# Reordering early loads and a store in a chunked state-space scan followed by a two-layer SiLU block

## The chip, the cores and the metric

The kernel runs on one core of a Trainium2 chip. The metric is the device time of one execution in microseconds (us), lower is better. TensorE (PE) multiplies matrices, VectorE (DVE), ScalarE (ACT) and GpSimd (POOL) do elementwise work, and SyncE (SP) mostly issues DMA transfers. Each engine works through its own queue in order.

## The reference

The first part is a Mamba-2 style scan over 4 batches, 8 heads, 768 positions, head size 32 and state size 16. For one chunk of positions:

```python
la = log(clip(a, 1e-6, 1.0)); cum = cumsum(la)
M = (C @ B.T) * exp(cum[:, None] - cum[None, :]) * causal
y = M @ x + (C @ state) * exp(cum)[:, None]
state = exp(sum(la)) * state + sum_j outer(B[j], x[j]) * exp(cum[-1] - cum[j])
```

The second part takes y as a matrix of 3072 tokens by 256 and computes `h = y @ w_in` (256 by 2048), `g = h * sigmoid(h)` and `out = g @ w_out` (2048 by 256). Everything is float32.

## The kernel before

The scan works in twelve units of 256 positions, three for each batch, numbered 0 to 11. Two units make one panel of 512 tokens for the second part, so there are six panels, P = 0 to 5. Panel 0 (units 0 and 1) is multiplied in plain float32 while its weights arrive; the later panels use weights and activations that are split into three parts, in the loop over `step(s)`. A hand-written order holds from the first instruction to the end of panel 0: the straight list of calls after the function definitions, then the list `steps`, then the texts "m0 ..." to "m5 ...". All engines receive their work in the order of these calls.

The weights come in sixteen blocks of 512 KB: blocks 0 to 7 of `w_in`, blocks 8 to 15 of `w_out`. This text counts them from 0, so "block five" in the short description of the change, which counts from one, is block 4. `load_w(n)` issues the load of block n on SP's queue into one of six buffers of the pool `quad`. `w_size(n)` is two ACT instructions that read the raw block (wu at L189, wv at L192). `w_bits(n)` is three DVE instructions and a POOL addition (L203 to L208) that give the usable block w. `f_s1(u, j)` multiplies block j with the scan result xf of unit u, eight matmuls (L531), and applies SiLU on ACT (gT, L534). Its PSUM tile hp has two buffers, so a product waits for the SiLU of the product before the last. `f_s2(j)` is the second layer of panel 0 (L544).

For a unit u of the scan: `f_TP` or `f_T` transposes B and C; `f_T2` makes ce from C (ACT, L408); `f_G` is the product of B and C (L442); scans over a on DVE give the decay matrix E (L356) and the prefix products pfx (L348); `f_B` scales B (BT, L380); `f_C` scales C (cw, L412); `f_D0` multiplies BT with x (L428); `f_M` (L448), `f_S` (L460, L462) and `f_SM` (L469) make the masked matrix and the states; `f_Y` (L482, L491) and `f_X` (L501) give xf. E and BT need the decays spread over partitions: for units 0 to 2 they come from products with `ach`, or from a copy `a_first`; from unit 3 on they come back from memory. For these POOL clamps a (`f_A2`, L273 and L275) after its load (`f_A1`), and `f_A3` stores it to the memory tensors `a_in` and `a_zero` with three SP issues (L280 to L282). `load_pa(u)` (L106) reads `a_in`, and `load_ab(u)` (L113) reads `a_zero` into ab, a tile with a single buffer, so it waits for the scans of the unit before. `load_n(u, i)` (L125) loads B (i = 0) or C (i = 1) with positions on partitions, `load_t` (L135) in another layout, `load_x` (L143) loads x, `load_bcx` both or some. `f_P0` (L344) clamps a for the prefix products of units 0 to 2 on POOL.

In the text of `steps`, each entry is `(u, j, work)`: first `f_s1(u, j)`, then the work, where `b3` is `w_bits(3)`, `s4` is `w_size(4)`, `r7` is `load_w(7)`, and `2:T2` calls `stage(2, ...)` with one letter for each function:

```python
steps = ((1, 0, "2:P1 s3"), (1, 1, "b3 s4 2:T2"), (0, 2, "2:BCa r7 b4 s5"), (1, 2, "2:DSsM r8 r9"),
```

In `stage` the letter `a` means `load_ab(u + 1)`.

Of the kernel before, what the change touches and what calls it, by code (L numbers as in the profile page):

```python
# [33 lines left out]
def kernel(  # L34
# [22 lines left out]
    nc = tc.nc  # L57
# [28 lines left out]
    def block(name, dtype=FP32):  # L86

        return blk.tile([128, 512], dtype, name=name, tag="blk", bufs=NB)
# [12 lines left out]
    def at(u):  # L101
        return u // UPB, u % UPB * UT

    def load_pa(u, q):
        PZ[u] = pz if u != 3 else block("pz3")[:, 0:4 * Q + 4].rearrange("p (c t) -> p c t", c=4)
        q.dma_start(out=PZ[u].rearrange("p c t -> p (c t)"),  # L106
                    in_=a_in[:, 4 * u - NC0:4 * u - NC0 + 4].rearrange("h (o c) t -> h o (c t)", o=1).to_broadcast([H, N, 4 * Q + 4]))

    def load_ab(u, q):
        ab[u] = loads.tile([128, 2, H, Q], FP32, name="ab")  # L110
        src, n = (a_first, 4 * u) if u < UPB else (a_zero, 4 * u - NC0)
        for c in range(2):
            q.dma_start(out=ab[u][64 * c:64 * c + 64].rearrange("p k h t -> p k (h t)"),  # L113
                        in_=src[n + c:n + 4:2].rearrange("(o k) h t -> o k (h t)", o=1).to_broadcast([64, 2, H * Q]))

    def load_n(u, i, q, ks=(0, 1)):
        b, t0 = at(u)
        if i == 1:
            if u not in tbc:
                tbc[u] = block("tbc0")[:, 0:256].rearrange("p (k h n) -> p k h n", k=2, h=H)  # L120
        elif u not in bn:
            bn[u] = (block("bn0")[:, 0:256].rearrange("p (k h n) -> p k h n", k=2, h=H) if u in (0, 1, 3) else
                     loads.tile([128, 2, H, N], FP32, name="bn"))
        for k in ks:
            q.dma_start(out=(bn, tbc)[i][u][:, k], in_=(B, C)[i][b, :, t0 + 128 * k:t0 + 128 * k + 128].rearrange("h p n -> p h n"))  # L125

    def load_t(u, i, q):
        b, t0 = at(u)
        if u == 0:
            tbc[u] = block("tbc0").rearrange("p (i e r n) -> p i e r n", i=2, e=2, r=8)  # L130
        elif u not in tbc:
            tbc[u] = loads.tile([128, 2, 2, 8, N], FP32, name="tbc")
        src = (B, C)[i]
        for g in range(4):
            q.dma_start(out=tbc[u][32 * g:32 * g + 32, i],  # L135
                        in_=src[b, 2 * g:2 * g + 2, t0:t0 + UT].rearrange("e (t r) n -> t e r n", r=8))

    def load_x(u, q, ks=(0, 1)):
        b, t0 = at(u)
        if u not in xt:  # L140
            xt[u] = loads.tile([128, 2, H, D], FP32, name="xt", bufs=2)
        for k in ks:
            q.dma_start(out=xt[u][:, k], in_=x[b, :, t0 + 128 * k:t0 + 128 * k + 128].rearrange("h p d -> p h d"))  # L143

    def load_bcx(u, what="bcx"):
        if "c" in what:
            if 0 < u < UPB:
                load_n(u, 1, nc.sync)
            else:
                load_t(u, 0, nc.sync)  # L150
                load_t(u, 1, nc.sync)
        if "b" in what:
            load_n(u, 0, nc.sync)
        if "x" in what:
            load_x(u, nc.sync)

    def load_unit(u):
        load_pa(u, nc.sync)
        load_bcx(u, "bc")
        load_ab(u, nc.sync)  # L160
        load_x(u, nc.sync)
# [10 lines left out]
    def two(t):  # L172
        return t.rearrange("p (k f) -> p k f", k=2)

    def load_w(n, q):
        j = n % 8
        src = wi[:, :, j * WF:(j + 1) * WF] if n < 8 else wo[:, 2 * j:2 * j + 2]
        if src.dtype == FP32:
            w32[n] = block("w32")
            q.dma_start(out=two(w32[n]), in_=src)  # L180
            return
        t = raw[n] = quad.tile([128, 2, WF, 2], U32, name="raw", tag="quad")
        q.dma_start(out=t.rearrange("p k f two -> p k (f two)"), in_=src.bitcast(U32))
# [86 lines left out]
    def f_A2(first):  # L270

        r = slice(0, NC1)
        nc.gpsimd.tensor_scalar(out=(acl if first else acz)[r], in0=acl[r], scalar1=1.0, scalar2=1e-6, op0=ALU.min, op1=ALU.max)  # L273
        if not first:
            nc.gpsimd.memset(acz[r, :, 0:1], 0.0)  # L275

    def f_A3():

        r = slice(0, NC1)
        nc.sync.dma_start(out=a_in[:, :, 0:1].rearrange("h c t -> c h t"), in_=misc[r, 0:H].rearrange("p (h t) -> p h t", t=1))  # L280
        nc.sync.dma_start(out=a_in[:, :, 1:].rearrange("h c t -> c h t"), in_=acl[r])
        nc.sync.dma_start(out=a_zero, in_=acz[r])  # L282
# [58 lines left out]
    def f_P0(u, engine):  # L341
        src = pa[u].rearrange("p (c t) -> p c t", t=Q)
        PZ[u] = (pz, pz1, pz)[u]
        engine.tensor_scalar(out=PZ[u][:, :, 1:], in0=src, scalar1=1.0, scalar2=1e-6, op0=ALU.min, op1=ALU.max)  # L344
# [16 lines left out]
    def f_Ab(u, k, hs=slice(0, H), bank=acc):  # L361
        t = ab[u, k, hs.start] = bank("ab").rearrange("p (h t) -> p h t", t=Q)
        nc.tensor.matmul(out=t[:, hs].rearrange("p h t -> p (h t)"),
                         lhsT=sel[:A1, 2 * u + k].rearrange("r c m -> r (c m)"),
                         rhs=ach[:A1, hs].rearrange("r h t -> r (h t)"), start=True, stop=True)
# [17 lines left out]
    def f_T(u, i):  # L383
        t = (BH, CT)[i][u] = sc.tile([128, UT], FP32, name=("bh", "ct")[i])
        nc.vector.transpose(out=t.rearrange("p (t r) -> p r t", r=8), in_=tbc[u][:, i].rearrange("p e r n -> p r e n"))
        if i == 1:
            tbc.pop(u)
# [17 lines left out]
    def f_T2(u, e):  # L405
        if e == 0:
            CE[u] = sc.tile([128, 2, UT], FP32, name="ce")
        nc.scalar.activation(CE[u][:, e], CT[u], AF.Copy, scale=par[:, e:e + 1])  # L408

    def f_C(u, engine=nc.vector):  # L410
        CW[u] = sc.tile([128, UT], FP32, name="cw")
        engine.tensor_tensor(out=CW[u].rearrange("p (c t) -> p c t", t=Q),  # L412
                             in0=CT.pop(u).rearrange("p (c t) -> p c t", t=Q), in1=PFX[u][:, :, 1:], op=ALU.mult)
# [32 lines left out]
    def f_M(u, k):  # L446
        m = E[u].rearrange("p k (g e) t -> p k g (e t)", e=2)
        nc.vector.tensor_tensor(out=m[:, k], in0=DP[u][:, :, 128 * k:128 * k + 128], in1=m[:, k], op=ALU.mult)  # L448
# [244 lines left out]
                in_=r[32 * q:32 * q + 32].rearrange("p (b d) -> p b d", d=32))  # L693


    f_P0(0, nc.gpsimd)
    load_n(1, 0, nc.gpsimd)
    f_Ab(0, 0, slice(0, 4))
    f_Ab(0, 0, slice(4, 8))
    f_Ab(0, 1, slice(0, 4), half)  # L700
# [24 lines left out]
    f_M(0, 0)  # L725
    w_size(0, "u")
    f_C(0, nc.gpsimd)
    load_n(1, 1, nc.gpsimd)
    f_S(0)
    f_SM(0)  # L730
    w_size(0, "v")
# [5 lines left out]
    busy(2)  # L737
    f_X(0)
    load_x(2, nc.sync)
    load_w(4, nc.sync)  # L740
    load_bcx(3, "c")
    load_w(5, nc.sync)
    f_P0(1, nc.gpsimd)
    w_bits(1, 2)
    f_s1(0, 0)
# [11 lines left out]
    f_P0(2, nc.gpsimd)  # L757
    f_A2(True)
    f_A2(False)
    f_M(1, 0)  # L760
    f_S(1)
    f_SM(1)
# [3 lines left out]
    f_Y(1)  # L766
    f_X(1)
    w_bits(2)
    f_A3()
    load_pa(3, nc.sync)  # L770
    load_n(3, 0, nc.sync)
    load_w(6, nc.sync)
    load_x(3, nc.sync)

    def stage(u, what):
        for c in what:
            if c == "L":
                load_unit(u)
            elif c == "a":
                load_ab(u + 1, nc.sync)  # L780
            elif c == "T":
                if 0 < u < UPB:
                    f_TP(u)
                else:
                    f_T(u, 0)
                    f_T(u, 1)
                f_T2(u, 0)
                f_T2(u, 1)
            elif c == "P":
                f_P(u)  # L790
            elif c in "12":
                f_E1(u, int(c) - 1, 2)
            elif c == "B":
                f_B(u)
            elif c == "C":
                f_C(u)
            elif c == "D":
                f_G(u)
                f_D0(u)
            elif c == "M":  # L800
                f_M(u, 0)
                f_M(u, 1)
            elif c == "S":
                f_S(u)
            elif c == "s":
                f_SM(u)
            elif c == "Y":
                f_Y(u)
                f_X(u)
            elif c == "h":  # L810
                f_xh(u)
            elif c == "l":
                f_xl(u)
            elif c == "d":
                f_xd(u)
# [4 lines left out]
    def todo(text):  # L820

        for step in text.split():
            if ":" in step:
# [3 lines left out]
            n = int(step[1:].split(".")[0])  # L827
            {"b": w_bits, "s": w_size, "h": w_h, "l": w_l, "d": w_d, "v": partial(w_d, vector=True), "m": f_s2, "p": s1_d, "r": load_r}[step[0]](n)

    steps = ((1, 0, "2:P1 s3"), (1, 1, "b3 s4 2:T2"), (0, 2, "2:BCa r7 b4 s5"), (1, 2, "2:DSsM r8 r9"),  # L830
             (0, 3, "b5 s6 r10"), (1, 3, "2:Y 3:T r11"), (0, 4, "3:P1 b6 s7 r12"), (1, 4, "3:C2B"), (0, 5, "b7 r13 s8"),
             (1, 5, "3:DSsM 2:h"), (0, 6, "b8 r14 s9 h0 l0"), (1, 6, "3:Y"), (0, 7, "b9 r15 s10 s11"), (1, 7, "b10 s12"))
    for u, j, text in steps:
# [119 lines left out]
```

## Time and profile before

| What | Value |
|---|---|
| Time, median of 3 runs | 339.26 us (336.94 to 339.36) |
| The profiled execution | 342.22 us, its span 340.3 us |
| PE busy | 325.5 us, 96% of the span |
| DVE busy | 250.0 us, 73% |
| ACT busy | 220.2 us, 65% |
| POOL busy | 81.8 us, 24% |
| Mean granted TensorE clock | 0.989 |
| Moved by DMA | 31.87 MB, mean 94 GB/s |

A busy share is an average over the span. The second section of the page cuts the span into 40 slices of 8.5 us and gives each engine's busy share in tenths for each, the granted clock of TensorE in tenths of full speed, and the mean busy share of the DMA engines. In a timeline a row has its start, its length, the engine and line, the operation, the tile written and the tiles read, how many instructions were merged, and in brackets how long the engine had been idle before it and what ended that. "SPq" is SP issuing a DMA; the transfer lands later.

### The profile page before, as it was taken

To read this page: it belongs to the slowest core of one execution; us is meant where nothing else is said; L and a number is where in the kernel's file an instruction comes from. 1 tells how busy PE (TensorE), PEld (TensorE's weight loads), DVE (VectorE), ACT (ScalarE), POOL (GpSimd) and SP (SyncE) were. 2 spreads that over 40 slices of the span, in tenths; PEclk is the share of its full clock that TensorE was granted. 3 is DMA by queue.
4 is the path that set the end of the run, shared out by engine and by line. 5 is a ranking of instruction groups with operands and counts; after the bars stand their busy time and mean duration, and the time that the engine had idled before them with its cause. 6 is when DMAs were issued, how large, how long until landed. Compare 5 with 4: busy or idle time off the path is not lost.

```text
span 340.3 us, 7984 instructions
## 1 busy us (share of the span) xinstructions
PE 325.5 (96%) x3222; PEld 261.6 (77%) x3225; DVE 250.0 (73%) x413; ACT 220.2 (65%) x422; POOL 81.8 (24%) x82
## 2 busy tenths in 40 slices
PE   8879849999999999999999999999999999999996
PEld 5558637788877878877778777778778778899996
DVE  7969556597778798898774898766897964494443
ACT  3555452993668889748766757775856676666662
POOL 6743211487501122043020333101231202000000
PEclk9999986999999999999999999999999999999999
DMA  6997694379787485263360163340163000002001
GB/s 138 238 163 184 137 319 174 94 165 209 134 172 123 102 154 95 54 118 48 79 111 0 35 121 61 71 93 0 47 110 64 2 2 0 0 14 51 2 0 62
DMA packets 90708, 31.87 MB, mean 94 GB/s; under 512 B 74432, under 2 KB 81344, under 8 KB 90672
## 3 DMA queue, kind: packets, MB, share of 16 engines
q1 hardware_dynamic: 85296, 25.47, 34.9%
q0 software_dynamic: 3008, 5.51, 9.3%
q10 hardware_dynamic: 2368, 0.39, 0.6%
q8 instruction: 25, 0.41, 0.5%
q14 instruction: 11, 0.09, 0.1%
HBM read 22.79 MB, written 3.32 MB: 77 GB/s over the span
## 4 chain that ended last, share of the span: by engine, by line
PE 82%; DMA 8%; SPq 3%; DVE 3%; ACT 2%; issue 1%; DVEq 0%
PE hp L567 23%; PE hp L559 11%; PE oa L608 9%; PE oa L609 9%; PE b L639 9%; PE oa L544 8%; DMA raw<-in_moe_w_in_dram 3%; DMA ab<-a_first 2%; PE b L634 2%; PE b L617 2%; PE oa L617 2%; PE gy L491 2%; PE gy L442 2%; PE hp L531 2%; DMA a_first<-ach 2%; PE gy L482 1%
## 5 line engine op out<-in xcount | busy, mean ns | idle before, releaser
L561 ACT ACTIVATE hp<-hp 128x512 f32<-128x512 f32 x80 | 46.6, 582 | 72.4 <-PE hp L559 72.4
L581 DVE TENSOR_TENSOR gl<-g,gh 128x512 fp32r<-128x512 f32 x62 | 42.7, 689 | 50.3 <-ACT gh L577 47.3
L567 PE MATMUL hp<-xh,wh 128*128 128x512 f32 x160 | 65.5, 409 | 0.0
L585 DVE SCALAR_TENSOR_TENSOR gd<-gh,g 128x512 fp32r<-128x512 f32 x80 | 59.5, 747 | 5.2 <-ACT gh L577 5.2
L567 PE MATMUL hp<-xl,wl 128*128 128x512 f32 x160 | 62.8, 393 | 0.0
L581 POOL TENSOR_TENSOR gl<-g,gh 128x512 fp32r<-128x512 f32 x18 | 29.2, 1621 | 122.2 <-ACT gh L577 122.2
L577 ACT ACTIVATE gh<-g 128x512 fp32r<-128x512 f32 x80 | 50.5, 632 | 2.8
L608 PE MATMUL oa<-gh,wh 128*128 128x512 f32 x128 | 50.1, 391 | 0.0
L609 PE MATMUL oa<-gl,wl 128*128 128x512 f32 x128 | 50.0, 391 | 0.0
L559 PE MATMUL hp<-xd,wd 128*128 128x512 f32 x160 | 49.6, 391 | 0.0
L575 ACT ACTIVATE g<-hp 128x512 f32<-128x512 f32 x80 | 47.4, 593 | 0.6 <-PE hp L567 0.6
L531 PE MATMUL hp<-xf,w 128*128 128x256 f32 x128 | 32.7, 405 | 7.3 <-ACT gT L534 6.8
L567 PEld LDWEIGHTS hp<-xh,wh 128*128 128x128 f32 x160 | 30.1, 188 | 8.8 <-ACT hp L561 2.5
L356 DVE TENSOR_TENSOR_SCAN E<-ab,diag 128x512 f32<-128x512 f32 (+1 forms) x26 | 30.5, 1205 | 7.4 <-DMA ab<-a_zero 6.6
L559 PEld LDWEIGHTS hp<-xd,wd 128*128 128x128 f32 x160 | 30.0, 188 | 6.8
L531 PEld LDWEIGHTS hp<-xf,w 128*128 128x128 f32 x128 | 24.3, 198 | 13.6 <-ACT gT L534 8.2
L639 PE MATMUL b<-gd,wd 128*128 128x512 f32 x128 | 34.6, 390 | 0.0
L567 PEld LDWEIGHTS hp<-xl,wl 128*128 128x128 f32 x160 | 30.1, 188 | 4.8
L208 POOL TENSOR_TENSOR w<-wu,wv 128x512 uint32<-128x512 uint32 (+1 forms) x18 | 24.9, 1384 | 32.5 <-DVE wv L206 32.5
L544 PE MATMUL oa<-gT,w 128*128 128x256 f32 x128 | 28.4, 379 | 0.0
L608 PEld LDWEIGHTS oa<-gh,wh 128*128 128x128 f32 x128 | 24.0, 188 | 5.2
L639 PEld LDWEIGHTS b<-gd,wd 128*128 128x128 f32 x128 | 24.0, 188 | 5.1
(103 smaller groups left out, 463.1 us busy)
## 6 DMA issues: line engine op xcount, KB each, us to landing
ab<-a_zero SPq DMA_DIRECT2D x18, 256.0 KB
raw<-in_moe_w_in_dram SPq DMA_DIRECT2D x8, 512.0 KB
raw<-in_moe_w_out_dram SPq DMA_DIRECT2D x8, 512.0 KB
wl<-w POOLq DMA_DIRECT2D x16, 256.0 KB, 4.4
xt<-in_x_dram SPq DMA_DIRECT2D x24, 128.0 KB
out_dram<-ot SPq DMA_DIRECT2D x40, 64.0 KB
tbc<-in_C_dram SPq DMA_DIRECT2D x40, 32.0 KB
bn<-in_B_dram SPq DMA_DIRECT2D x20, 64.0 KB
```

The costliest lines, as they stand in the source:

```text
L531: nc.tensor.matmul(out=hp[:, i], lhsT=two(w32[j])[:, kc, 128 * i:128 * i + 128], rhs=two(XF[u])[:, kc], start=(kc == 0), stop=(kc == KC - 1))
L544: nc.tensor.matmul(out=OA[0][m][:, UT * u:UT * u + UT], lhsT=two(w32[8 + j])[:, i, 128 * m:128 * m + 128], rhs=two(GT[u, j])[:, i], start= ...
L559: nc.tensor.matmul(out=HP[s], lhsT=two(WD[f // 2])[:, kc, 128 * (f % 2):128 * (f % 2) + 128], rhs=XD[P][:, kc], start=(kc == 0), stop=Fals ...
L561: nc.scalar.activation(HP[s], HP[s], AF.Copy, scale=HALF / UP)
L567: nc.tensor.matmul(out=HP[s], lhsT=two(w[f // 2])[:, kc, 128 * (f % 2):128 * (f % 2) + 128], rhs=x_[P][:, kc], start=False, stop=(kc == KC ...
L575: nc.scalar.activation(G[s], HP.pop(s), AF.Silu, scale=UP)
L577: nc.scalar.activation(GH[s], G[s], AF.Copy, scale=DOWN)
L581: engine.tensor_tensor(out=GL[s], in0=G[s], in1=GH[s].bitcast(FP32), op=ALU.subtract)
L585: nc.vector.scalar_tensor_tensor(out=GD[s], in0=GH[s].bitcast(FP32), scalar=1.0 + 1.0 / HALF, in1=G.pop(s), op0=ALU.mult, op1=ALU.subtract)
L608: nc.tensor.matmul(out=OA[P][m], lhsT=two(WH[n])[:, r, ms], rhs=gh, start=(f == 0), stop=False)
L609: nc.tensor.matmul(out=OA[P][m], lhsT=two(WL[n])[:, r, ms], rhs=gl, start=False, stop=(f == NF - 1))
L639: nc.tensor.matmul(out=B2[P][:, m], lhsT=two(WD[n])[:, r, 128 * m:128 * m + 128], rhs=gd, start=(fresh and s == tiles[0]), stop=True, skip ...
```

## The change

The change moves calls in the hand-written order; no computation is added or left out. On POOL's queue the two loads of B of unit 1 go ahead of the first clamp `f_P0(0)`, and the two loads of C of unit 1 ahead of the product `f_C(0)`. On SP's queue the three stores of `f_A3` go ahead of the loads of blocks 4 and 5, which now stand together after POOL's `f_A2`, followed by B and C of unit 3 and the load of block 6, and then by `load_pa(3)`. The load of the zeroed a of unit 3 and of block 7 move from the entry (0, 2) of `steps` to the entry (1, 1), and B and x of unit 3 go behind them, through two new letters, `n` and `x`. In the order of SP's queue:

- before: x of 2, block 4, B and C of 3, block 5, three stores, p of 3, B of 3, block 6, x of 3, zeroed a of 3, block 7, block 8
- after: x of 2, three stores, block 4, block 5, B and C of 3, block 6, p of 3, zeroed a of 3, block 7, B of 3, x of 3, block 8

("B and C of 3" in the layout of `load_t`; "B of 3" in that of `load_n`.)

```diff
+    load_n(1, 0, nc.gpsimd)
     f_P0(0, nc.gpsimd)
-    load_n(1, 0, nc.gpsimd)
+    load_n(1, 1, nc.gpsimd)
     f_Ab(0, 0, slice(0, 4))
...
     f_C(0, nc.gpsimd)
-    load_n(1, 1, nc.gpsimd)
     f_S(0)
...
     load_x(2, nc.sync)
-    load_w(4, nc.sync)
-    load_bcx(3, "c")
-    load_w(5, nc.sync)
     f_P0(1, nc.gpsimd)
...
     f_A2(True)
     f_A2(False)
+    f_A3()
+    load_w(4, nc.sync)
+    load_w(5, nc.sync)
+    load_bcx(3, "c")
+    load_w(6, nc.sync)
+    load_pa(3, nc.sync)
     f_M(1, 0)
...
     w_bits(2)
-    f_A3()
-    load_pa(3, nc.sync)
-    load_n(3, 0, nc.sync)
-    load_w(6, nc.sync)
-    load_x(3, nc.sync)
...
+            elif c == "n":
+                load_n(u, 0, nc.sync)
+            elif c == "x":
+                load_x(u, nc.sync)
...
-    steps = ((1, 0, "2:P1 s3"), (1, 1, "b3 s4 2:T2"), (0, 2, "2:BCa r7 b4 s5"), (1, 2, "2:DSsM r8 r9"),
+    steps = ((1, 0, "2:P1 s3"), (1, 1, "b3 s4 2:T2a r7"), (0, 2, "2:BC 3:nx b4 s5 r8"), (1, 2, "2:DSsM r9"),
```

## The prediction

> **What bounds the kernel now.** I read the page first: engines, then slices.
>
> ```profile
> span 340.3 us, 7984 instructions
> PE 325.5 (96%) x3222; PEld 261.6 (77%) x3225; DVE 250.0 (73%) x413; ACT 220.2 (65%) x422; POOL 81.8 (24%) x82
> PE   8879849999999999999999999999999999999996
> PEclk9999986999999999999999999999999999999999
> DMA  6997694379787485263360163340163000002001
> ```
>
> A slice is 8.5 us. From the eighth on PE is full, and the chain that ended last holds almost only PE pieces after 65.97: everything there is paid in PE work, which the change does not touch. Only slices 1 to 8 have holes. In slices 6 and 7 the holes are deepest, and there alone the granted clock falls. So I next read the waits from 15 to 85 us (engine, line, releaser: total, times, longest):
>
> ```profile
> ACT wu L189 <- DMA raw<-in_moe_w_in_dram: 10.8, 4, 4.6
> PE hp L531 <- ACT gT L534: 6.8, 5, 3.5
> DVE E L356 <- DMA ab<-a_zero: 6.6, 1, 6.6
> ```
>
> PE waits for gT, ACT's SiLU of a first-layer product. ACT, in order, is stuck before it in wu, the first step on a newly loaded weight block. The timelines of SP's queue, ACT and PE put times on this:
>
> ```profile
> 24.79 0.94 SPq L183 DMA_DIRECT2D raw<-in_moe_w_in_dram  x1
> 30.48 0.43 SPq L183 DMA_DIRECT2D raw<-in_moe_w_in_dram  x1
> 37.40 1.01 SPq L183 DMA_DIRECT2D raw<-in_moe_w_in_dram  x1
> 39.64 2.49 SPq L113 DMA_DIRECT2D ab<-a_zero  x2
> 42.23 0.54 SPq L183 DMA_DIRECT2D raw<-in_moe_w_in_dram  x1
> ...
> 41.65 0.66 ACT L189 ACTIVATE wu<-raw 128x512 f32<-128x512 f32 x1 [4.64 <-DMA raw<-in_moe_w_in_dram]
> 49.02 0.67 ACT L189 ACTIVATE wu<-raw 128x512 f32<-128x512 f32 x1 [3.84 <-DMA raw<-in_moe_w_in_dram]
> ...
> 32.58 0.70 PE L442 MATMUL gy<-ce,bh 32*64 32x128 f32 x32
> 43.40 3.88 PE L531 MATMUL hp<-xf,w 128*128 128x256 f32 x16 [2.07 <-ACT gT L534]
> 50.77 3.78 PE L531 MATMUL hp<-xf,w 128*128 128x256 f32 x8 [3.48 <-ACT gT L534]
> 54.48 1.16 PE L442 MATMUL gy<-ce,bh 32*64 32x128 f32 x32
> ```
>
> Loads 4, 5, 6, 7 (counted from 0) are issued at 24.79, 30.48, 37.40, 42.23. Load 6 lands at 41.65, load 7 at 49.02, the zeroed a of unit 3 at 46.28; all three are waited for.
>
> What can be won: from 32.58 (the G product of unit 2) to 56.17 (first product with block 6) PE needs 23.59 us. Its own work there: six first-layer products of 8 matmuls at 1.9, 11.4 (0.1 more than half of the 3.62 to 3.72 that sixteen take elsewhere); G and D of units 2 and 3 at 0.98 and 1.08; Y of unit 2 1.41: 14.9. The other **8.7** is 0.44 + 2.07 + 3.48 of waits, 1.9 by which the product at 50.77 is too slow, 0.7 in G and D after it (1.16 and 0.68 for 0.70 and 0.46).
>
> Those last 2.6 come from the clock: the granted clock is 1.00 up to 48, 0.83 in 48 to 50, 0.50 in 50 to 56. The Trainium skill ("TensorE: Matmul & The Clock Gate", the HAM clock gate) says that an idle window of about 3.4 us halves the clock. The trace agrees: 3.48 halved it, 2.07 did not. The rule also speaks against this change, below.
>
> **The change part by part.**
>
> *B and C of unit 1 on POOL.* B's two issues (2.07 us) move from 6.63 to about 3.95, into the 2.26 us in which POOL waited for the first a; the issues end at 6.02, and the clamp behind them, at 6.18, waits for that landing anyway. C's issues (1.81) move from 9.33 to 6.6 and end at about 8.45; the product cw behind them starts at 8.70, when its prefix scan ends (8.61). POOL pays nothing. C's landing held PE's transposes by 0.31 and 0.62. Without that, G of unit 1 starts when ce is ready, about 17.7 for 18.90; D then waits for BT (POOL, 17.61 to 18.51, behind the DVE scan), so 18.55 for 19.52. Gain at this place about 0.95. Price: 0.26 MB enters DMA engines that were busy anyway, ahead of load 0, which ACT awaits at 9.34 with 0.18 us to spare before the state's mask. At the 227 to 342 GB/s there, 0.26 MB is up to 1.1 us. So -0.95 to +0.9; I take -0.95, and it hardly matters, see load 4.
>
> *Stores of a ahead of load 4.* SP's three issues (30.96 to 32.31) go in behind x of unit 2 (ends 24.74). They wait for POOL's clamps, done at 22.88 and 23.90: no wait. They cost SP 1.35, so load 4 goes from 24.79 to **26.15**. It landed 4.9 after issue (ACT found it at 29.69); so at 31.05. Behind it on ACT are bh, ce and gT: from wu to the end of ce is 2.23 us (29.69 to 31.92), so ce ends at 33.3 and G of unit 2 starts at 33.4, **0.8 later** than 32.58. PE then idles from about 31.5 to 33.4. The early 0.95 is lost in that wait: the landing decides. Bounds: 4.2 (load 6's flight) to 6.8 (load 7's) gives 30.3 to 33.0.[...]
>
> Here the clock rule bites: 1.9 us idle stays under its window, as 2.07 did in the trace. If load 4 lands past 32.6 the gap reaches 3.5 and costs another 2.6.
>
> *Loads 5, 6, p and zeroed a of unit 3, load 7.* Load 5 goes directly behind load 4, at 26.6 for 30.48. Each SP load also waits until the one eight before it has landed (the order of the program shows this ring of eight semaphores). So the last two loads of C of unit 3 wait for loads 4 and 5: 31.1 and about 32.5. Load 6 follows at about **33.2** for 37.40 (its buffer has been free since load 0 was converted at 13.2), p at 33.8, and zeroed a at 34.4 for 39.64: its single buffer is free after unit 2's second scan (30.85, here about 29.9), so SP does not stop. With its own 2.49, load 7 at 37.0 for 42.23, then B of unit 3 (1.08) and x (1.04) by 39.2, load 8 at about 39.8 for 42.86. B and x, now behind load 7, land around 44 by the 4 to 7 us of their neighbours; BT wants B at 46.6.
>
> Landings with the old flights: load 6 33.2 + 4.25 = 37.5; zeroed a 34.4 + 6.6 = 41.0; load 7 37.0 + 6.8 = 43.8.
>
> *PE from 33.4.* G and D to 34.4; (0,3) to 36.3; (1,3), released by gT at 35.7, to 38.2; Y to 39.6; (0,4) 41.5; (1,4) needs gT of (1,3), which stands behind load 6's wu and wv on ACT: 37.5 + 1.1 + 0.6 = 39.2, no wait. (1,4) to 43.4; (0,5) 45.3. (1,5) needs gT of (1,4), behind load 7's wu and wv: 43.8 + 1.1 + 0.6 = 45.5, **0.2 late**. It ends at 47.4 at full clock. G needs ce, long done; D needs BT: scan 41.0 to 42.2, block 6's three DVE steps to 43.7, cw 44.1, second scan 2.3, BT 46.8: in time. First product with block 6 at 48.5 to **48.7**, for 56.17: **7.5 earlier**. As a sum: 8.7 of waits and slow clock, less 0.8 (load 4), less 0.2 (load 7), less 0.2 for rounding and issue gaps = 7.5.
>
> *From there to 65.97.* The 9.8 us are set by D, M, block 8's DVE steps, xh, then ACT's run of eleven steps to gT of (1,7), all behind the same D of unit 3, and 0.22 and 0.59 of PE wait. They move as one. Loads 8 to 11 were issued from 42.86 on, held by the eight-ring; they move 3 us and are wanted at 46 (load 8; behind load 7 at about 330 GB/s it needs 1.6 us more, 45.4) and 53.6 (load 9). Loads 12 to 15 are released by the DVE steps on blocks 6, 7, 9, 10, which move too. After 65.97 PE has its fixed queue: p0 at 82.88 wants xd at 79.91 and ACT waits 5.3 us for PE, so the feeders have 3 us to spare and move along.
>
> Profiled execution: 342.22 around a span of 340.3; 342.22 - 7.5 = 334.7. The median of the runs is 2.96 below the profiled one; I take the same difference off it: 339.26 - 7.5 = **331.8**.
>
> **Rivals.**
>
> *A, load 4 cools PE.* Load 4 past 32.6 (6.5 us flight; load 7 had 6.8 under heavier traffic, load 6 4.25): gap 3.5, clock halved. Gain 7.5 - 1.6 - 2.6 = 3.3: 336.0. For it: two 512 KB loads and three stores now leave together while B and x of unit 2 still drain (DMA share 1.03, 0.96 in 24 to 28). Against: the share falls to 0.53 and 0.39 at 28 to 32.
>
> *B, more goes.* Load 4 lands by 30.3 and the early 0.95 survives, and the 0.8 of PE waits near 61 to 64 go: 7.5 + 0.8 + 0.95 + 0.8, about 10: 329.3.
>
> *C, the feeders do not follow.* ACT is full from 60.16 to 78.49, and blocks 8 to 15 must come 7.5 earlier. If loads 9 to 11 arrive at the old times PE waits in the second layer and half is given back: 335.5. Against: these were issued from 42.86 on, and ACT took load 9 at 61.17 without a wait.
>
> *D, slower: the ring of eight.* Everything behind C of unit 3 now hangs on load 5's landing. Issue of load 6 to load 7 is 3.8 us against 4.8, so from a load 5 landing after 37.7 on (11 us of flight) load 7 is later than before and every further us is lost: at 13 us of flight that is 1.9: 341.2. Against: load 5 flew 3.7 (ACT found it at 34.21), and no load in the trace 11.
>
> That the moves do nothing is excluded by the program's order: the queues of SP and POOL differ as said.
>
> **How the numbers follow.** Forecast 0.60, A 0.14, B 0.10, C 0.10, D 0.06. Range: forecast with its bounds 330 to 334, B below, A above: 328.8 to 336.5, leaving out D and half of C and A's tails. A measurement here tells 1% (3.4 us) from none: faster than 335.9 holds the forecast, B, half of A and C: 0.82; within 1%: 0.12; slower: 0.06.
>
> **What would show it.** Right: SP issues load 6 near 33 and load 7 near 37; ACT's waits before wu fall from 4.64 and 3.84 to under 1 each, with a new one of 1 to 2 at block 4; DVE's wait for zeroed a falls from 6.6 to about 2; granted clock 1.00 in 48 to 56; first second-layer matmul near 58.4 for 65.80, and PE gapless after. Wrong: a half clock anywhere after 31, load 6 issued after 36, or PE waits between 58 and 85.

## The result, and the profile after

| | before | changed |
|---|---|---|
| median, nine runs each | 339.09 us (336.94 to 339.87) | 334.43 us (333.16 to 336.32) |
| profiled execution / its span | 342.22 / 340.3 us | 335.11 / 333.1 us |

The ratio is 0.987, 95% interval 0.984 to 0.990: the change makes the kernel faster, by 1.0 to 1.6%. The two medians differ by 4.66 us, the two profiled executions by 7.11. The forecast of 7.5 for one profiled execution was nearly met, the forecast of 331.8 for the median was 2.6 too low, though inside the stated range. That gap is the main question below.

The page of the changed kernel, its span, engine totals and slices of 8.3 us:

```profile
span 333.1 us, 7989 instructions
PE 323.3 (97%) x3225; PEld 262.2 (79%) x3225; DVE 250.1 (75%) x413; ACT 220.6 (66%) x422; POOL 82.0 (25%) x82
PE   8979898999999999999999999999999999999996
PEclk9998999999999999999999999999999999999999
DMA  6996885698994683164420164410253000012001
```

The hole of PE in slice 6 (4 tenths before, 9 now) is gone, and so is the half clock of slices 6 and 7. What is new is a granted clock of 8 tenths in slice 4; the 7 tenths of PE in slice 3 were there before. The waits from 15 to 85 us (engine, line, releaser: total, times, longest):

```profile
ACT wu L189 <- DMA raw<-in_moe_w_in_dram: 1.6, 1, 1.6
PE hp L531 <- ACT gT L534: 0.8, 2, 0.6
...
DVE E L356 <- DMA ab<-a_zero: 0.3, 1, 0.3
```

ACT waits once for a block of the first layer, 1.6 us for 10.8; PE waits 0.8 for gT instead of 6.8; DVE 0.3 for the zeroed a instead of 6.6. The timelines of SP, ACT and PE of the same execution give the times:

```profile
26.26 0.91 SPq L183 DMA_DIRECT2D raw<-in_moe_w_in_dram  x2
...
33.24 0.39 SPq L183 DMA_DIRECT2D raw<-in_moe_w_in_dram  x1
...
34.39 1.26 SPq L113 DMA_DIRECT2D ab<-a_zero  x2
35.75 0.53 SPq L183 DMA_DIRECT2D raw<-in_moe_w_in_dram  x1
...
37.76 5.79 SPq L143 DMA_DIRECT2D xt<-in_x_dram  x2
43.64 17.33 SPq L183 DMA_DIRECT2D raw<-in_moe_w_out_dram  x8
...
31.62 0.69 ACT L189 ACTIVATE wu<-raw 128x512 f32<-128x512 f32 x1 [1.57 <-DMA raw<-in_moe_w_in_dram]
...
37.89 0.67 ACT L189 ACTIVATE wu<-raw 128x512 f32<-128x512 f32 x1
42.95 0.70 ACT L189 ACTIVATE wu<-raw 128x512 f32<-128x512 f32 x1
47.83 0.68 ACT L189 ACTIVATE wu<-raw 128x512 f32<-128x512 f32 x1 [0.51 <-DMA raw<-in_moe_w_out_dram]
...
24.30 5.11 PE L531 MATMUL hp<-xf,w 128*128 128x256 f32 x16 [0.47 <-ACT xf L501]
...
34.38 0.70 PE L442 MATMUL gy<-ce,bh 32*64 32x128 f32 x32 [1.07 <-DVE cw L412]
...
49.35 3.72 PE L531 MATMUL hp<-xf,w 128*128 128x256 f32 x16
...
59.00 17.43 PE L544 MATMUL oa<-gT,w 128*128 128x256 f32 x80
```

Loads 4 and 5 leave together at 26.26, load 6 at 33.24, load 7 at 35.75. Blocks 6 and 7 are taken at 37.89 and 42.95 without a bracket: they had landed. G of unit 2 starts at 34.38, the first product with block 6 at 49.35, the second layer at 59.00.

From the first second-layer matmul to the end of the span it is 274.5 us before (65.80 to 340.3) and 274.1 after. In the traces of all twelve experiments it is 274.0 to 274.5. So of the 7.2 us between the two spans 6.8 arise before that matmul, and its time stands for the kernel's to within half a microsecond.

### The profile page after: what moved, and what is told of

Its sections match the earlier page's. It is cut to its first block, busy times and chain, and to the rows that moved or that the text cites. A ratio compares the mean times of both kernels' runs of the same rounds, so it can differ in the third digit from the quotient of the medians.

```text
span 333.1 us, 7989 instructions
## 1 busy us (share of the span) xinstructions
PE 323.3 (97%) x3225; PEld 262.2 (79%) x3225; DVE 250.1 (75%) x413; ACT 220.6 (66%) x422; POOL 82.0 (25%) x82
## 4 chain that ended last, share of the span: by engine, by line
PE 88%; DMA 5%; SPq 2%; ACT 2%; DVE 1%; issue 1%
PE hp L567 23%; PE hp L559 11%; PE oa L608 9%; PE oa L609 9%; PE b L639 9%; PE oa L544 8%; PE hp L531 4%; PE b L634 2%; PE b L617 2%; PE oa L617 2%; PE gy L491 2%; DMA a_first<-ach 2%; PE gy L442 2%; PE gy L482 2%; DMA raw<-in_moe_w_in_dram 2%; DMA ab<-a_first 1%
## 5 line engine op out<-in xcount | busy, mean ns | idle before, releaser
L559 PE MATMUL hp<-xd,wd 128*128 128x512 f32 x160 | 49.6, 391 | 0.0
L531 PE MATMUL hp<-xf,w 128*128 128x256 f32 x128 | 31.4, 397 | 2.7 <-ACT xf L501 1.2
L609 PEld LDWEIGHTS oa<-gl,wl 128*128 128x128 f32 x128 | 24.0, 188 | 5.1
```

What stands on the lines that cost most here:

```text
L531: nc.tensor.matmul(out=hp[:, i], lhsT=two(w32[j])[:, kc, 128 * i:128 * i + 128], rhs=two(XF[u])[:, kc], start=(kc == 0), stop=(kc == KC - 1))
L559: nc.tensor.matmul(out=HP[s], lhsT=two(WD[f // 2])[:, kc, 128 * (f % 2):128 * (f % 2) + 128], rhs=XD[P][:, kc], start=(kc == 0), stop=Fals ...
L609: nc.tensor.matmul(out=OA[P][m], lhsT=two(WL[n])[:, r, ms], rhs=gl, start=False, stop=(f == NF - 1))
```

## The experiments

Each was timed in five rounds against runs of the kernel before on the same chip. The first and the eleventh are unchanged kernels, for the spread.

Two theories of the gap between 7.1 and 4.7 were put up. The first: the shown execution of before was slower than usual, and its waits are smaller as a rule. The second: it was usual, and the rest of the kernel varies.

**The kernel before again** (no edit).

> The kernel before, unchanged, executed again. Theory 1 (its shown execution, 342.22 us, was about 3 us slower than its usual one; the waits for loads 6 and 7 and the half clock after them are smaller as a rule): a new execution takes 337 to 340 us, PE waits less than 3.4 us ahead of product (1,5), and the time at half clock after it is shorter or absent. Theory 2 (the shown execution was usual, and the rest of the kernel varies): the new execution shows again about 2.1 and 3.5 us of wait and about 6 us at half clock. Both: timed against itself, a ratio of 1.

Measured: 338.46 us (337.29 to 339.75), ratio to the same kernel 0.9973, interval 0.9946 to 0.9999. That is the resolution here: nothing was changed, and the interval still just leaves out 1, so a ratio of 0.997 is no difference. The runs of before beside it: median 339.25, 337.48 to 342.32, so the shown 342.22 stands at their upper end. The traced execution took 338.83. Three of its stretches of 2 us (the length, busy time of PE, PEld, DVE, ACT, POOL with counts, then granted clock, DMA share, GB/s) and its PE and ACT timelines:

```profile
20.00:22.00 2.00, 0.19 (x1) 0.01 (x1) 1.77 (x6) 1.01 (x3) 0.69 (x2) 1.00 1.03 214
22.00:24.00 2.00, 1.98 (x96) 1.88 (x96) 1.68 (x4) 0.82 (x2) 1.37 (x3) 0.50 0.78 74
...
50.00:52.00 2.00, 2.00 (x13) 1.13 (x19) 1.93 (x4) 0.29 (x2) 0.00 (x0) 0.50 1.04 403
...
24.74 5.73 PE L531 MATMUL hp<-xf,w 128*128 128x256 f32 x16 [0.47 <-ACT xf L501]
...
48.71 3.23 PE L531 MATMUL hp<-xf,w 128*128 128x256 f32 x8 [2.62 <-ACT gT L534]
...
40.44 0.68 ACT L189 ACTIVATE wu<-raw 128x512 f32<-128x512 f32 x1 [2.54 <-DMA raw<-in_moe_w_in_dram]
46.94 0.67 ACT L189 ACTIVATE wu<-raw 128x512 f32<-128x512 f32 x1 [2.96 <-DMA raw<-in_moe_w_in_dram]
```

Here the clock halves at 22, after PE had waited 1.83 us for the masked matrix M of unit 1 (DVE, L448); the sixteen matmuls of two products take 5.73 us instead of 3.72. ACT so comes 1.8 us later to load 4, which it finds landed, and 0.9 us later to load 6, for which it waits 2.54 us instead of 4.64. And the landings are earlier: load 6 is taken at 40.44 for 41.65, load 7 at 46.94 for 49.02. SP had issued load 7 only 0.46 us earlier (41.77 for 42.23); why it was also on its way 1.6 us less, the traces do not show. The second half clock is shorter. From load 7's wu to the first product with block 6 it is 6.34 us (46.94 to 53.28), before 7.15. Second layer at 62.90, for 65.80. The 2.9 us between the two traces of one kernel are 2.08 from load 7's landing and 0.8 from what follows it, the shorter half clock above all. The first theory holds on the size; that the usual execution has a shorter half clock held only in part, since it has an additional one at 22.

**The part on POOL alone.**

```diff
+    load_n(1, 0, nc.gpsimd)
     f_P0(0, nc.gpsimd)
-    load_n(1, 0, nc.gpsimd)
+    load_n(1, 1, nc.gpsimd)
...
     f_C(0, nc.gpsimd)
-    load_n(1, 1, nc.gpsimd)
```

> Only the part on POOL: B and C of unit 1 issued ahead of the first clamp and of C's product; SP's order as before. Prediction's reading: G of unit 1 0.4 to 0.95 us earlier, then swallowed by the landings of loads 4 to 7, so the time stays within 0.5 us of before. Rival, from the trace of the changed kernel (loads 1 and 2 and the stored first a 1.2 to 1.5 us later): SP runs later from load 2 on, loads 6 and 7 land up to 1 us later, and the kernel is up to 1 us slower.

Measured: 338.61 us, ratio 0.9991 (0.9964 to 1.0018): no difference. Its G of unit 1 stands at 19.18, against 18.90 and 18.14 in the two traces of before: the spread between executions of one kernel, 0.76, is nearly as large as the 0.95 that I had claimed.

**The part on SP alone** (the whole change without those lines).

> Only the part on SP: the stores of a ahead of load 4, loads 5, 6, zeroed a and 7 earlier, B and x of unit 3 behind load 7; POOL's order as before. If the gain is all in the landings of loads 6, 7 and zeroed a: 334 to 335 us, as the whole change. If the POOL part carries a share of it (SP reaches the loads of unit 2 earlier since C of unit 1 is out of the way): 335 to 337 us.

Measured: 334.04 us, ratio 0.9851 (0.9820 to 0.9882). So the gain lies in the part on SP; the whole change's 0.987 cannot be told from it. What each move inside this part gives alone was not measured, but for the two experiments on load 6 and on the stores below.

**PE kept busy in the wait for load 7**, in the kernel before.

```diff
     for u, j, text in steps:
+        if (u, j) == (1, 5):
+            busy(14, 0, acc("zero"))
         f_s1(u, j)
```

> The kernel before with 14 matmuls on zeros (3.0 us at 0.216 each) put on PE ahead of product (1,5), into the wait for load 7; they write a bank that nothing reads. Where the wait is 3.5 us they cost nothing and keep the clock: product (1,5) takes 1.9 instead of 3.8, in all 2.6 us less. If the half clock is the smaller cause in a usual execution (shorter wait), the gain is under 1 us or a loss of up to 1 us.

Measured: 338.35 us, ratio 0.9974 (0.9946 to 1.0003), as the unchanged kernel beside it. In the trace the clock is 1.00 from 46 to 58, product (1,5) takes 1.89 and G of unit 3 0.69: the half clock was taken away, and less than the resolution came of it (by the interval, at most 1.8 us). In a usual execution the 2.6 us that I had read from one trace are not to be had there. The matmuls also outlasted the wait a little: gT was done at 49.6, PE went on at 50.03.

**Only load 6 ahead of p of unit 3**, in the kernel before.

```diff
     f_A3()
+    load_w(6, nc.sync)
     load_pa(3, nc.sync)
     load_n(3, 0, nc.sync)
-    load_w(6, nc.sync)
```

> The kernel before with one move: load 6 ahead of p of unit 3, the load that waits for the store of a to land (SP stood there from 31.5 to 34.7). Theory: this stop of 3.2 us held load 6, and only load 6 gains: issued near 31.6 for 36.6, landing near 36 for 40.4, so ACT does not wait for it; but p, zeroed a and load 7 stay where they were (load 7 lands near 47), and PE waits there longer: 1 to 2.5 us faster than before, 336.5 to 338. Rival, that load 6 is the whole matter: 334 to 335.

Measured: 338.41 us, ratio 0.9988 (0.9960 to 1.0016): no difference, less than either view expected. SP's timeline and ACT's wait for load 7:

```profile
34.03 0.40 SPq L183 DMA_DIRECT2D raw<-in_moe_w_in_dram  x1
37.39 0.63 SPq L106 DMA_DIRECT2D pz<-a_in  x1
...
43.31 0.53 SPq L183 DMA_DIRECT2D raw<-in_moe_w_in_dram  x1
...
49.24 0.69 ACT L189 ACTIVATE wu<-raw 128x512 f32<-128x512 f32 x1 [4.29 <-DMA raw<-in_moe_w_in_dram]
```

Load 6 leaves ahead of the stop and is not waited for (its wu at 39.79 has no wait). But p still waits for the store to land (34.43 to 37.39), and zeroed a and load 7 stand behind it. ACT's wait moved from load 6 to load 7. Load 6 alone gives nothing that can be measured; by the traces, what counts is when load 7 and the zeroed a leave. These two were not moved apart from each other. In the second trace of before, BT of unit 3, which needs the zeroed a, is done at 51.45, and D, which needs BT, starts at 52.87: load 7 sets the time there, and the zeroed a would take over once load 7 is about 1.4 us earlier (an estimate from these two times).

**The stores behind loads 4 and 5** (with the part on SP).

```diff
-    f_A3()
     load_w(4, nc.sync)
     load_w(5, nc.sync)
+    f_A3()
     load_bcx(3, "c")
```

> Only the part on SP, with the three stores of a behind loads 4 and 5 instead of ahead of them. If the stores ahead of load 4 cost what the prediction put on them (1.35 us of issue, load 4 later, G of unit 2 0.8 later) and nothing needs them so early: up to 0.8 us faster than the SP part alone, 333.3. If p and zeroed a of unit 3 need the stores early (the ring of eight, the read after the store): load 6 stays, zeroed a lands 1 us or more later, 334.5 to 336.

Measured: 335.19 us, ratio 0.9885 (0.9850 to 0.9920), which overlaps the SP part's interval; SP issues load 6 at 33.50 and load 7 at 36.02, about as with the stores first. Neither view is shown: the 0.8 us that I put on the stores ahead of load 4 did not come back, and no loss is shown either. Here too the stores stand well ahead of p; which side of loads 4 and 5 is better for them is not resolved.

**PE kept busy ahead of Y of unit 1**, against the half clock at 22: in the changed kernel, in the SP part, and in the SP part with the stores later.

```diff
-    busy(4)
+    busy(12)
     f_Y(1)
```

> The changed kernel with 12 instead of 4 matmuls on zeros ahead of Y of unit 1 (8 more, 1.7 us, into PE's wait of 1.84 there). If the half clock at 22 to 27 us costs the changed kernel its 1.4 us (16 products in 5.11 instead of 3.72): 333.0. If load 4's landing (31.6) covers it, as PE's wait of 1.07 ahead of G of unit 2 in the trace says: less than 0.5 us, 334.

> Only the part on SP, with the same 8 additional matmuls on zeros. Its trace without them shows load 4 landed before ACT asked (30.47) and no wait ahead of G of unit 2, so here the half clock (16 products in 5.27 instead of 3.72) lies on the path: 1 to 1.5 us less than the SP part alone, 332.5 to 333. If load 4 then becomes the wait (landing near 31): 333.5 to 334.

> The SP part with the stores of a behind loads 4 and 5, and 8 more matmuls on zeros ahead of Y of unit 1. Theory (half clock at 22 to 31 us on the path where load 4 is early; load 4's landing on the path where it is late): load 4 leaves near 24.8 and lands near 29.5, ACT wants it at 29, so no second half clock, and the 16 products take 3.7 for 6.2: 2 us less than with the stores later alone, 332.5 to 333.5. Rival (load 4 still lands near 31 to 32 as in the kernels with the matmuls before): a wait of 2 us or more ahead of G of unit 2, half clock there, 335.

Measured: 335.12 us, ratio 0.9897 (0.9844 to 0.9950); 335.05, 0.9882 (0.9827 to 0.9936); 334.78, 0.9872 (0.9829 to 0.9914). None is faster than without the matmuls; the second was to gain 1 to 1.5 and did not. The traces of the first and third say where the time goes; that of the second is of its slowest execution, 338.61, and is left out. The changed kernel with the matmuls, one execution of 337.72, PE, ACT and one stretch:

```profile
24.56 3.72 PE L531 MATMUL hp<-xf,w 128*128 128x256 f32 x16 [0.47 <-ACT xf L501]
...
34.92 1.16 PE L442 MATMUL gy<-ce,bh 32*64 32x128 f32 x32 [2.74 <-DVE cw L412]
...
36.59 6.01 PE L531 MATMUL hp<-xf,w 128*128 128x256 f32 x16
...
32.22 0.66 ACT L189 ACTIVATE wu<-raw 128x512 f32<-128x512 f32 x1 [3.30 <-DMA raw<-in_moe_w_in_dram]
...
34.00:36.00 2.00, 1.08 (x32) 0.76 (x32) 1.53 (x4) 2.00 (x6) 0.00 (x0) 0.61 0.52 139
```

The first sixteen matmuls run at full clock. ACT then asks for load 4 at 28.92 and gets it at 32.22; PE stands 2.74, the clock halves there instead, and the next sixteen matmuls take 6.01. Two other executions of this kernel took 332.94 and 333.40, and another 337.91; whether load 4's landing tells them apart is not shown, since they have no trace. With the stores later the clock is 1.00 from 20 to 58 throughout, and the time shows up as ACT's waits for loads 6, 7 and 8:

```profile
37.19 0.70 ACT L189 ACTIVATE wu<-raw 128x512 f32<-128x512 f32 x1 [1.27 <-DMA raw<-in_moe_w_in_dram]
42.77 0.69 ACT L189 ACTIVATE wu<-raw 128x512 f32<-128x512 f32 x1 [1.79 <-DMA raw<-in_moe_w_in_dram]
47.67 0.68 ACT L189 ACTIVATE wu<-raw 128x512 f32<-128x512 f32 x1 [2.66 <-DMA raw<-in_moe_w_out_dram]
```

**Load 4 ahead of x of unit 2** (with the part on SP), without and with the additional matmuls.

```diff
-    load_x(2, nc.sync)
+    load_w(4, nc.sync)
...
     f_A3()
-    load_w(4, nc.sync)
+    load_x(2, nc.sync)
     load_w(5, nc.sync)
```

> The SP part with load 4 ahead of x of unit 2, without the additional matmuls. Theory: load 4 off the path, the half clock at 22 to 28 us on it, 1.4 to 2.6 us: 334 to 335, 1.5 to 2.5 more than with the matmuls. Rival, that the half clock costs nothing: the same time as with them.

> The SP part with load 4 ahead of x of unit 2 (issued near 22.5 to 23.5 for 26.5), then the stores, x of unit 2, load 5, and 8 more matmuls on zeros ahead of Y of unit 1. Theory: load 4 lands by 29, no wait ahead of G of unit 2, full clock through 22 to 60: 331.5 to 333. Rival: x of unit 2, now behind the 512 KB, or the ring of eight takes the wait over (D of unit 2 late by 1 us or more): 334 to 335.

Measured: 334.55 us, ratio 0.9867 (0.9826 to 0.9909), and 334.76, 0.9874 (0.9831 to 0.9916). The rival held, that the half clock costs nothing here: with the matmuls the clock is 1.00 from 20 to 58, without them 0.61 and 0.53 in 24 to 28, and the time is the same. In the trace of the version with the matmuls ACT waits 0.95, 2.52, 1.57, 1.21 and 2.26 for loads 4 to 8; without them for none of these. What PE gains early, ACT waits out at the next loads in these two traces.

**The changed kernel again** (no edit).

> The changed kernel, unchanged, on this chip, beside the others. Expected: 334 to 335 us. If the part on POOL is worth nothing, within 0.5 us of the SP part alone (334.04); if it costs what it delays at load 2 (1.4 us in SP's queue), 335.

Measured: 335.50 us, ratio 0.9891 (0.9835 to 0.9946). Its six executions go from 333.71 to 339.83, so the changed kernel has longer executions too. Whether the part on POOL costs a little is not resolved. In this trace load 4 is taken at 30.14 (31.62 in the first), G of unit 2 starts at 33.36, and the second layer at 57.17, 1.8 earlier than in the first trace of the same kernel.

No version beats the changed kernel by more than the comparison resolves; the SP part alone, at 334.04, has the lowest median.

## Why the prediction was right, and where it was off

**Right: the cause and its steps, for the execution it was worked from.** Load 4 was to leave at 26.15 and left at 26.26; load 6 at 33.2, left at 33.24; zeroed a was to land at 41.0 and released DVE at 41.35. From G of unit 2 to the first product with block 6 I had 15.1 to 15.3 us, almost all of it PE's own work; it took 14.97 (34.38 to 49.35), before 23.59. From there to the second layer it took 9.65, before 9.63: the feeders followed, and rival C fell. The second layer was to begin at 58.4 and began at 59.00. The sum 7.5 came out as 7.11 between the profiled executions.

Two readings behind it were a little off. The 14.97 hold 0.65 us in which PE stood at 43.7 with no wait that the profile names; two traces below without such a gap took 14.15 and 14.16, so PE's own work was about 0.7 less than my 14.9. And on the page only slice 6 had a hole of PE; slice 7 was full, at a lowered clock (6 tenths).

**The step that failed: "I take the same difference off it".** The 7.5 was made against one execution of 342.22 and carried to the median as if its waits were those of every execution. They were not. The term that was too large for a usual execution is "the other 8.7" of waits and slow clock. The stretch that it was read from, in the traces with SP's order of before and of the change:

| Trace | G of unit 2 | first product with block 6 | between | second layer |
|---|---|---|---|---|
| before, the one shown | 32.58 | 56.17 | 23.59 | 65.80 |
| before again | 34.29 | 53.28 | 18.99 | 62.90 |
| before, the part on POOL | 35.34 | 53.15 | 17.81 | 62.77 |
| changed | 34.38 | 49.35 | 14.97 | 59.00 |
| changed again | 33.36 | 47.51 | 14.15 | 57.17 |
| the part on SP | 33.94 | 48.10 | 14.16 | 57.75 |

In the two other traces with the old order the stretch is 4.6 to 5.8 us shorter than in the one shown; it also starts 1.7 to 2.8 later, behind a half clock between 22 and 30 that the one shown did not have. The second layer is thus 2.9 and 3.0 earlier. 7.5 less 2.9 is 4.6, and the medians differ by 4.66; that these agree so closely is chance, for between the second traces of the two kernels it is 5.73 (62.90 to 57.17). I noted that the shown execution lay 2.96 above the median, and treated this as an offset outside the stage at issue. It lay in that stage, in the late landing of load 7 and the longer half clock behind it, and the change removes just those. Why load 7 landed so late in that execution stays open.

**Off: load 4.** Its landing was put at 31.05 and came at 31.6 (5.3 us of flight for 4.9). G of unit 2 came at 34.38 for 33.4: 0.55 from the landing and 0.42 from cw (DVE), which in this trace stands behind ce (it starts at 33.90, after a wait of 0.83 for ce) and which I left out of the sum. In the second trace of the changed kernel it left at 25.09 and was taken at 30.14, 5.0 later. The bounds of 4.2 to 6.8 us of flight hold both. In that second trace the condition of rival B was met, load 4 by 30.3, but not its gain: the half clock (0.87, 0.50 and 0.78 in 22 to 28) made PE itself late, and G came at 33.36.

**Off: load 7 and load 8.** Zeroed a took SP 1.26 instead of 2.49, so load 7 left at 35.75 for 37.0 and ACT did not wait for it; the 0.2 that I had put on it did not occur. Load 8 was to leave at 39.8 and land at 45.4. It left at 43.64, because the two issues of x took SP 5.79 us, and ACT waited 0.51 for it at 47.83. I had 1.04 for these two issues, from a row with less traffic.

**Off: B and C on POOL.** G of unit 1 came at 18.46 for 18.90, 0.44 earlier instead of 0.95, with load 1 taken at 12.65 for 11.39 and load 2 issued at 10.15 for 8.79: the price that I had bounded was paid. That it hardly matters was right: alone, the part shows no difference.

**Off: the clock rule.** I took 1.9 and 2.07 us of PE wait as safe. In the new trace of before the clock halved at the end of a wait of 1.83. In the changed kernel it halved about 1.4 us behind one of 1.84 (0.93, 0.50, 0.71 in 22 to 28; 0.93 puts it near 23.7), while after 1.83 at the same place in the shown execution it stayed at 1.00. Ahead of product (1,5), 2.62 us in the new trace of before and 2.19 with the part on POOL were followed by half clock (0.50 and 0.59 in 50 to 52). All these are well under the 3.4 us that I took as the bound; the measurement decides, and no safe length is shown here. The half clock at 22 to 28, which the forecast did not have, did not reach the end in the first trace of the changed kernel, where PE waited 1.07 ahead of G of unit 2 for what hung on load 4. Rival A, a half clock at G of unit 2, did not occur in either trace of the changed kernel; it did occur once PE came early (the matmuls ahead of Y). Rival D, the ring of eight, did not occur: SP waited 2.4 us in all for loads 4 and 5 at the last loads of C of unit 3, as the prediction's issue times for them imply, and load 6 left as forecast.

## What to carry to other kernels

A gain read as the sum of waits in one profiled execution held here for that execution only; if it lies above the median of the other runs, ask first whether the surplus sits in the stage that the change repairs, and take it off the gain. A load that waits for a store to land stops every load behind it in that queue (3.2 us here, at p of unit 3). Here it paid to move the store forward and, with it, the loads that the engines ask for next; moving only the first load moved the wait to the next. Whether moving the store alone would do was not tried.

## What the runs showed of the hardware

The granted clock of TensorE can halve after a wait of only 1.83 us, and the same wait left it alone in another execution. Matmuls on zeros in that wait kept it at 1.00 from 20 to 34 in the three traces told of here, where the traces without them had about 0.50 for some 3 to 7 us; in one of them it halved later, at a wait of 2.74. They saved nothing that could be measured; in these traces ACT waited for loads instead.

SP needed 5.79 us to issue two loads of x with runs of 128 bytes while loads 6, 7 and zeroed a were on their way, and 4.0 to 6.3 in all nine traces with that order; in the kernel before the same two issues took 1.04, and 1.04 to 1.42 in the five traces with the old order. Load 8, next in the queue, left at 43.64, where the forecast had 39.8.
